# One core, attention with compressive memory beside a spectral filter: token-stage layout of W, folded back transform, merged masks, reciprocals through TensorE, and a new order

## The chip, the core and the metric

The kernel runs on one core of a Trainium2 chip. The core has five engines with a queue each: TensorE (PE, matrix products into the accumulation memory PSUM), VectorE (DVE), ScalarE (ACT), GpSimd (POOL) and SyncE (SP, which here only issues DMA transfers). Work memory is SBUF, 128 partitions wide. Inputs are in the chip's main memory (DRAM in the code). The metric is the device time of one execution in microseconds; lower is better. The kernel before takes 242.37 us, the median of three runs (241.94 to 242.49).

## The reference, cut to what matters

Two branches are computed from `x` (2048 tokens, width 640) and mixed by a gate per token:

```python
g = sigmoid((x * gate_w).sum(-1, keepdims=True))
# branch a: 32 heads of width 20, four segments of 512 tokens
for s in range(4):
    logits = einsum('bhqd,bhkd->bhqk', qs, ks) * scale + mask
    p = softmax(logits)
    a_dot = einsum('bhqk,bhkd->bhqd', p, vs)
    a_mem = einsum('bhld,bhde->bhle', phi(qs), M) / (einsum('bhld,bhd->bhl', phi(qs), z) + 1e-6)
    o = sigmoid(beta) * a_mem + (1 - sigmoid(beta)) * a_dot
    M, z = M + phi(ks)^T vs, z + sum(phi(ks))
a = o @ wo
# branch b
b = irfft2(rfft2(x) * (w_r + 1j * w_i))
out = g * a + (1 - g) * b
```

The mask is causal inside a segment. Softmax is done without its maximum: exponentials are taken, cells above the diagonal are set to zero, and the product with V carries a column of ones, whose result is the denominator.

## The kernel before

A recording layer (`Sched`) takes the whole kernel as some 2,000 operations, each with the buffers it reads and writes. The tuple `ORDER` says in which order they go to which engine, `ENDED` in which order they are thought to end; both are written out as numbers. Each engine then runs its own list strictly in order, and semaphores carry every dependence between engines. PSUM has eight banks: four for the scores of attention (`qk`), four for all else (`gen`). One scores unit takes all four `qk` banks, so the next unit's products start only when ACT has taken the exponentials of the one before.

Branch a, per segment `s`: `proj_tile` projects Q and K and sends them through main memory into a padded layout (`st_qk`, `pad`), `v_part` projects V, `qk_unit` makes scores in five units for a pair of head groups and takes their exponentials into `ex` (line 1393, ACT), and `mask` zeroes cells with POOL's affine select (line 1414), seven calls for each of 32 head groups, each as soon as its unit's exponentials are there. `pv_flipped` (segments 0 to 2) multiplies with V and sends the result, denominators included, to main memory (`st_u`, tile `u_scr`); `pv_group` does it for segment 3 without that detour. `mem_read_tile` reads the memory: a product, a denominator, a reciprocal and a multiplication for each half of the heads (lines 1281 to 1289, DVE). `denominators` (line 1331) loads the denominators back (`ld_den`), takes reciprocals on DVE (`den_rec`, line 1340), multiplies by the gate (`den_gate`, line 1342, tile `rc`) and stores them (`st_r`, tile `r_scr`). `finish_tile` then loads them back with each row repeated four times (`ld_r`, tile `r`), multiplies the attention result by them (`normal`, line 1656), adds the memory part (line 1664), and accumulates the product with `wo` (line 519) in the same PSUM bank as the last step of branch b.

Branch b, in `fft` (line 1495), is a two-dimensional real transform as matrix products. Stage F1 transforms over 128 of the token index. Stage D transforms over the width (tile `Bt`). Then comes the token stage, for 16 groups `g`: products T give real and imaginary parts, `W_mul` (line 1569, DVE) multiplies each of two PSUM results by `w_r` and `w_i` at once, `W_add` (line 1574, DVE or POOL) adds or subtracts the four products into `Yt`, and products Tb transform back, three chunks of the width by two, 256 columns each (tile `Cp`). The back transform over the width (Db) is, for each of 16 values of `n2` and for cosine and sine, three products of 321 columns; DVE adds and subtracts the two results into the two halves of `G` (`sum_Db`, line 1615), since cosine is even and sine is odd. The last step over the tokens (Fb) multiplies `G` by a table with the gate in it, into the bank of the `wo` product. Tables `tt` and the rows of W (`Wt`, double buffered, 32 transfers of 80 KB) come from main memory for each pair of groups.

SP issues nearly all transfers, in order; a transfer whose data are not ready holds all that stand behind it. All in all PE, DVE, ACT, POOL and SP run 1073, 481, 249, 293 and 232 recorded operations.

Of the kernel before, what the change touches and what calls it, by code (L numbers as in the profile page):

```python
# [8 lines left out]
ALU = mybir.AluOpType  # L9
# [35 lines left out]
class Op:  # L45
    __slots__ = ("id", "alts", "preds", "succs", "prio", "banks", "nbytes", "npred", "eng", "t0", "t1",
                 "stamp", "rank", "need_inc", "dyn", "first", "outside", "name", "dma", "key", "xfer", "lock", "mode", "emode", "hold", "width")


class Sched:  # L50
# [9 lines left out]
    def op(self, alts, r=(), w=(), prio=0.0, nbytes=0, name="", after=(), dma=False, xfer=0.0, lock=False, mode=0, hold=False, width=16):  # L60
# [3 lines left out]
        o = Op()  # L64
        o.id = len(self.ops)
# [46 lines left out]
    def schedule(self, pools, order, ended, nsem=56):  # L112
# [12 lines left out]
        for o in ops:  # L125
            o.dyn, o.t1 = [], None
            o.first = [b for b in o.banks if b.ops[0] is o]
            for b in o.banks:
                b.left = len(b.ops)
        pe, held = queue["pe"], {}  # L130
# [42 lines left out]
        def head(e):  # L173
# [4 lines left out]
            for p in o.preds:  # L178
                if p.t1 is None:
                    return None  # L180
                if p.eng != "pe" or e != "pe":
                    t = max(t, p.t1 + self.HOP)
            if o.first:
# [18 lines left out]
        while len(self.order) < len(order):  # L202
# [15 lines left out]
            o.t0 = t  # L218
            occ, lat = o.alts[e][1:]
# [95 lines left out]
def make_tables():  # L315
# [5 lines left out]
    for g in range(16):  # L321
        for i in range(4):
            a = 2 * pi * base_of(g, i) * n1 / 128
            F[:, g, i, 0], F[:, g, i, 1] = np.cos(a), -np.sin(a)
            Fp[g, i, 0], Fp[g, i, 1] = np.cos(a), np.sin(a)
# [23 lines left out]
    dd = np.arange(KD)  # L349
    IC = np.zeros((384, 322))  # L350
    IS = np.zeros((384, 322))
    IC[:KD, :KD] = ck[:, None] * np.cos(2 * pi * kd[:, None] * dd[None] / D)
    IS[:KD, :KD] = ck[:, None] * np.sin(2 * pi * kd[:, None] * dd[None] / D)
    IS[0] = 0
    IS[320] = 0
    IS[:, 320] = 0

    T = np.zeros((16, 128, 4, 128))
    Tp = np.zeros((16, 128, 2, 2, 16, 4, 2))
    n2 = np.arange(16)  # L360
    k2 = np.arange(16)
    for g in range(16):
        for half in range(2):
            for i in range(4):
                kb, pi_, kind, sg = pair_of(g, half, i)
                k = kb + 128 * k2
                ph = 2 * pi * np.outer(n2, k) / S
                c, s = np.cos(ph), np.sin(ph)
                m = half * 64 + k2 * 4 + i
                kr = n2 * 8 + pi_ * 2  # L370
                ki = kr + 1

                def put(t, rows, val):
                    T[g, rows[:, None], t, m[None, :]] = val
                if kind == "pair":
                    put(0, kr, c), put(0, ki, sg * s), put(1, kr, -s), put(1, ki, sg * c)
                    put(2, kr, -s), put(2, ki, sg * c), put(3, kr, -c), put(3, ki, -sg * s)
                else:
                    src = kr if kind == "zero" else ki
                    put(0, src, c), put(1, src, -s), put(2, src, -s), put(3, src, -c)  # L380

                def putp(r, typ, eo, val):
                    for q in range(16):
                        Tp[g, m[q], r, typ, :, pi_, eo] = val[:, q]
                if kind == "pair":
                    putp(0, 0, 0, c), putp(1, 0, 0, -s), putp(0, 0, 1, -sg * s), putp(1, 0, 1, -sg * c)
                    putp(0, 1, 0, -s), putp(1, 1, 0, -c), putp(0, 1, 1, -sg * c), putp(1, 1, 1, sg * s)
                else:
                    eo = 0 if kind == "zero" else 1
                    putp(0, 0, eo, c), putp(1, 0, eo, -s), putp(0, 1, eo, -s), putp(1, 1, eo, -c)  # L390

    def chunks(t):
        return np.ascontiguousarray(t.reshape(3, 128, -1).transpose(1, 0, 2))
    fcat = np.concatenate([F, np.eye(128), Fp], 1)
    inv = np.concatenate([chunks(IC), chunks(IS)], 1).reshape(128, 6 * 322)
    big = np.concatenate([dtab, inv], 1)
    hmask = np.zeros((128, 5, 8, VW))
    for t in range(5):
        for r in range(128):
            hmask[r, t, (128 * t + r) // DH - head0(t), :DH + 1] = 1.0  # L400
    b = ml_dtypes.bfloat16
    return {"fcat": fcat.astype(b), "big": big.astype(b),
            "tt": np.concatenate([T.reshape(16, 128, 512), Tp.reshape(16, 128, 512)], 2).astype(b),
            "hmask": hmask.reshape(128, 880).astype(b)}
# [7 lines left out]
def pair_of(g, half, i):  # L412

    if g == 0:
        if half == 0:
            return 32 * i, i % 2, ("zero", "pair", "nyq", "pair")[i], (1, 1, 1, -1)[i]
        return 16 + 32 * i, (3, 2, 2, 3)[i], "pair", (1, 1, -1, -1)[i]
    if half == 0:
        return g + 32 * i, i, "pair", (1, 1, -1, -1)[i]
    return 32 - g + 32 * i, 3 - i, "pair", (1, 1, -1, -1)[i]  # L420
# [48 lines left out]
class Kern:  # L469
# [79 lines left out]
    def dma(self, dst, src, nbytes, r, w, prio, tr=False, name="", after=(), queue="sp"):  # L549
# [13 lines left out]
        "ld_W": (620.0, 450.0, 16), "ld_beta": (400.0, 120.0, 16), "ld_big": (500.0, 2900.0, 16), "ld_den": (520.0, 150.0, 16),  # L563
        "ld_fcat": (400.0, 350.0, 16), "ld_g": (400.0, 1500.0, 16), "ld_gc": (580.0, 200.0, 16), "ld_gw": (420.0, 600.0, 16),
        "ld_hm": (600.0, 850.0, 16), "ld_r": (570.0, 500.0, 16), "ld_tt": (530.0, 1650.0, 16), "ld_u": (500.0, 450.0, 16),
# [4 lines left out]
        "st_part": (430.0, 250.0, 16), "st_r": (480.0, 200.0, 16), "st_u": (520.0, 700.0, 16), ("xT", 131072): (1240.0, 1300.0, 16), ("xT", 262144): (1700.0, 2300.0, 16),  # L570
# [1166 lines left out]
```

## Time and profile before

| what | before |
|---|---|
| device time, median of 3 runs | 242.37 us |
| the profiled execution: span, first to last instruction | 247.9 us |
| PE busy in the span | 230.0 us (93%) |
| DVE, ACT, POOL busy | 196.3, 199.7, 165.7 us |
| mean granted clock of TensorE | 0.972 |
| bytes moved by DMA | 42.11 MB |

The profile gives no time of the profiled execution beside its span; the span is 5.5 us longer than the median of the runs. A row of the page or of a view names a line of the code, the engine, the operation, the tile written and the tiles read, and how often; then come busy time and the mean of one in ns, and the idle time of the engine ahead of it with what ended it. Products overlap on PE, so the mean of one is longer than what one adds to a row of them. In the timelines the numbers are the start and the length in us of a stretch of equal instructions.

### The profile page before, as it was taken

Reading aid. Unit: us, or ns where it says so; the run is one execution under the profiler, and the core shown is the slowest. Engines: PE = TensorE matmul, PEld = TensorE weight load, DVE = VectorE, ACT = ScalarE, POOL = GpSimd, SP = SyncE. Lnnn points to the kernel's source line nnn. Section 1 sums busy time; section 2 is a strip of 40 time slices with the busy share of each in tenths; the row PEclk is TensorE's granted clock in tenths of the full one; section 3 lists DMA queues with packets and bytes.
Section 4 is the critical chain, followed back from the end, with each engine's and each line's share of the span. In section 5 each row is a group of like instructions: output and inputs, shape, how many; then the busy total and the mean of one; then the engine's idle time right before and its main releaser. Section 6 shows DMA issues by size and latency. Waiting matters only on the chain.

```text
span 247.9 us, 9233 instructions
## 1 busy us (share of the span) xinstructions
PE 230.0 (93%) x3849; PEld 139.7 (56%) x3849; DVE 196.3 (79%) x481; ACT 199.7 (81%) x241; POOL 165.7 (67%) x297
## 2 busy tenths in 40 slices
PE   7899999999999999998899999999999975699994
PEld 2574667765465665545566554455444543366794
DVE  0489998799999987888998979979888831755653
ACT  2289688998999989999999899999999864278740
POOL 8532278367969658478939998949898660559640
PEclk9999999999999999999999999999999995599999
DMA  7999979937875864768697543447665977382123
GB/s 174 281 361 206 229 191 230 269 91 203 222 173 163 199 213 114 206 95 252 170 242 208 165 131 99 122 146 192 188 183 128 282 101 81 35 118 81 59 81 109
DMA packets 58924, 42.11 MB, mean 170 GB/s; under 512 B 30020, under 2 KB 55172, under 8 KB 58884
## 3 DMA queue, kind: packets, MB, share of 16 engines
q1 hardware_dynamic: 57844, 40.96, 66.4%
q8 instruction: 30, 0.49, 0.8%
q10 hardware_dynamic: 1040, 0.57, 0.8%
q14 instruction: 10, 0.08, 0.2%
HBM read 23.32 MB, written 12.30 MB: 144 GB/s over the span
## 4 chain that ended last, share of the span: by engine, by line
PE 59%; DVE 15%; DMA 12%; ACT 8%; SPq 3%; issue 2%; DVEq 0%
PE psum L521 52%; PE psum L519 6%; ACT ex L1393 5%; DMA r<-r_scr 3%; DMA r_scr<-rc 3%; DVE Pt L1569 3%; DMA Wt<-in_B_w_i_dram 2%; DMA wk<-in_A_wk_dram 2%; DMA qk_scr<-qu 2%; SPq L553 2%; DVE G L1615 1%; SPq L555 1%; DVE oU L1656 1%; DVE phk L1213 1%; DVE va L1244 1%
## 5 line engine op out<-in xcount | busy, mean ns | idle before, releaser
L1393 ACT ACTIVATE ex<-psum 128x2048 bf16<-128x2048 f32 (+4 forms) x92 | 138.7, 1507 | 13.2 <-PE psum L521 11.4
L1414 POOL TENSOR_SCALAR_AFFINE_SELECT ex<-ex 128x256 bf16<-128x256 bf16 (+2 forms) x224 | 121.0, 562 | 41.2 <-ACT ex L1393 38.3
L521 PE MATMUL psum<-qkp 20*64 20x64 bf16 (+5 forms) x1024 | 31.8, 268 | 4.0 <-ACT ex L1393 2.1
L521 PE MATMUL psum<-xT,wk 128*128 128x256 bf16 (+1 forms) x280 | 33.9, 273 | 0.6 <-DMA wk<-in_A_wk_dram 0.6
L521 PE MATMUL psum<-xT,wq 128*128 128x512 bf16 (+1 forms) x135 | 30.7, 381 | 0.5 <-DMA xT<-in_A_x_dram 0.5
L521 PE MATMUL psum<-wv,xT 128*64 128x320 bf16 (+3 forms) x240 | 30.1, 303 | 0.3 <-DVE va L1244 0.3
L1569 DVE TENSOR_TENSOR Pt<-psum,Wt 128x642 bf16<-128x642 f32 x32 | 25.5, 821 | 2.6 <-PE psum L521 1.5
L521 PEld LDWEIGHTS psum<-qkp 20*64 20x64 bf16 (+1 forms) x1024 | 12.2, 101 | 22.0 <-ACT ex L1393 14.8
L521 PEld LDWEIGHTS psum<-xT,wk 128*128 128x128 bf16 (+1 forms) x280 | 19.9, 97 | 7.1 <-DMA wk<-in_A_wk_dram 1.6
L519 PE MATMUL psum<-wo,oU 128*32 128x320 bf16 x480 | 23.5, 317 | 0.2 <-DVE oU L1664 0.2
L1035 POOL TENSOR_TENSOR xsb<-xf 128x320 bf16<-128x320 bf16 (+2 forms) x12 | 9.5, 788 | 16.2 <-DVE xsb L1035 12.2
L1244 DVE TENSOR_TENSOR va<-psum,ebx 128x320 bf16<-128x320 f32 x32 | 15.2, 483 | 5.0 <-ACT gate L1242 2.9
L521 PEld LDWEIGHTS psum<-wv,xT 128*64 128x64 bf16 (+1 forms) x240 | 14.9, 105 | 7.4 <-issue 2.9
L532 DVE CAST ot<-psum 128x320 bf16<-128x320 f32 x21 | 10.1, 491 | 11.2 <-PE psum L519 8.8
L521 PE MATMUL psum<-big,Cp 128*128 128x321 bf16 (+1 forms) x96 | 18.7, 310 | 0.2 <-DVE G L1615 0.2
L521 PE MATMUL psum<-big,Ac 128*128 128x160 bf16 (+2 forms) x96 | 18.1, 257 | 0.3 <-DVE Pt L1569 0.2
L521 PE MATMUL psum<-ex,va 128*32 128x512 bf16 (+4 forms) x480 | 17.3, 275 | 0.5 <-DVE mem L1289 0.2
L521 PE MATMUL psum<-tt,Yt 128*128 128x256 bf16 (+1 forms) x96 | 16.5, 276 | 1.1 <-DVE Pt L1569 0.4
L1615 DVE TENSOR_TENSOR G<-eo,psum 128x320 bf16<-128x320 f32 x32 | 14.7, 482 | 3.5 <-PE psum L521 2.5
L1201 ACT ACTIVATE et<-qu 128x512 bf16<-128x512 bf16 x25 | 15.6, 629 | 0.2
L519 PEld LDWEIGHTS psum<-wo,oU 128*32 128x32 bf16 x480 | 12.5, 100 | 5.7 <-issue 1.1
L521 PEld LDWEIGHTS psum<-ex,va 128*32 128x32 bf16 x480 | 10.1, 96 | 9.8 <-POOL ex L1414 1.7
(99 smaller groups left out, 393.7 us busy)
## 6 DMA issues: line engine op xcount, KB each, us to landing
qkp<-qk_scr SPq DMA_DIRECT2D x28, 160.0 KB
tt<-tab_tt SPq DMA_DIRECT2D x8, 512.0 KB, 3.8
qk_scr<-qu SPq DMA_DIRECT2D x12, 256.0 KB, 2.4
u_scr<-ub SPq DMA_DIRECT2D x12, 256.0 KB, 4.4
xsb<-in_A_x_dram SPq DMA_DIRECT2D x8, 320.0 KB, 5.9
oU<-u_scr SPq DMA_DIRECT2D x15, 128.0 KB, 4.0
out_dram<-ot SPq DMA_DIRECT2D x12, 160.0 KB
Wt<-in_B_w_r_dram SPq DMA_DIRECT2D x16, 80.2 KB, 3.3
```

The lines of the kernel that those rows point to most:

```text
L519: h = e.matmul(dst, wt, r_, start=st, stop=sp_, **{**kw, "tile_position": (0, q), "skip_group_check": True})
L521: h = e.matmul(o_, l_, r_, start=st, stop=sp_, **kw)
L532: alts["dve"] = (lambda e: e.tensor_copy(dst(), src()), 67 + 1.04 * n, 68.0)
L553: return e.dma_start_transpose(d_, s_)
L555: return e.dma_start(d_, s_)
L1035: self.either(lambda e, dst=dst, src=src, d0=d0, n=n, op=op: e.tensor_tensor(xs.ap(o + dst, [D, 2], [1, n]), xf.ap(src + d0, [321, 2], [1, ...
L1201: self.one("act", lambda e: e.activation(et.ap(0, [1, L]), qsl(), ACT.Exp), L, [qb], [b("et", pi_)], late, name="phi_exp")
L1244: self.one("dve", lambda e: e.tensor_tensor(va.ap(i * H * VW + h0 * VW, [VW, nh], [1, DH]), self.ps(bank, 0, [DH, nh], [1, DH]), self.ebx. ...
L1393: self.one("act", lambda e, d=d, q=q: e.activation(self.ex.ap(*d), self.ps(bank, *q), ACT.Exp, scale=SC), n, [bank], [self.exb(s, 2 * pr + ...
L1414: self.one("pool", lambda e: e.affine_select(self.ex.ap(e0 + d0, [1280, 4], [1, n], np_=np_), self.ex.ap(e0 + s0, [1280, 4], [1, n], np_=np_),
L1569: self.one("dve", lambda e, ri=ri, Pt=Pt, Wt=Wt, wo_=wo_, bank=bank: e.tensor_tensor(Pt.ap(ri * 322, [644, 2], [1, KD]), self.ps(bank, 0, ...
L1615: self.one("dve", lambda e, q=q, n2=n2, bank=bank, eo=eo: e.tensor_tensor(self.G.ap(n2 * D + 639 * q, [1 - 2 * q, 320]), eo.ap(q, [1, 320] ...
```

## The change

1. **Token stage.** `W_add` and the tile `Yt` are gone. The tables are laid out so that real parts stand in partitions 0 to 63 and imaginary parts in 64 to 127; then the sums over real and imaginary parts happen inside the back products, which take the W products `Pt` themselves as weights: 192 products Tb of 128 columns in the place of 96 of 256, written in runs of four PSUM columns out of eight, with weights at every second column of `Pt`. The pairs of groups are ordered anew (`GROUPS`).
2. **W.** Both halves of the partitions need the same rows of W. They are loaded from main memory into partitions 0 to 63 and copied to 64 to 127 by one transfer inside SBUF (`dup_W`), which waits for the loads.
3. **Back transform.** Db is folded a second time: even and odd `kd` separately, 161 outputs each. Two products of 161 columns and one of 322 take the place of three of 321. `sum_Db` writes to a new f32 tile `UV`; a new operation `fold_Db` (32 times, DVE or POOL) makes `G` from it. Fb takes `G` in two pieces of 161 and 159 columns, the second backward: 256 products for 128.
4. **Masks.** Seven calls for a head group become four, made after all of its exponentials. Each covers two blocks; on DVE it is one `min` against a table of 0 and very large numbers, on POOL two affine selects. `ORDER` puts 66 of the 128 on DVE.
5. **Reciprocals.** `st_r`, `r_scr` and `ld_r` are gone. Four products with 0/1 tables spread `rc` over the partitions in PSUM (`spread`), and a copy brings it to SBUF (`ev_r`).
6. **Smaller ones.** `mem_read_tile` takes one reciprocal of 32 columns for two of 16. `phi_max` may run on POOL (15 of 30 do). The first piece of `wk` is issued by ACT's queue. `on` and `xf` lie elsewhere in SBUF; one of the fills of `va` comes after the folds.
7. **Order.** `ORDER` and `ENDED` are new throughout.

```diff
@@ mask
-        self.one("pool", lambda e: e.affine_select(
-            self.ex.ap(e0 + d0, [1280, 4], [1, n], np_=np_), self.ex.ap(e0 + s0, [1280, 4], [1, n], np_=np_),
...
+        least = lambda e: e.tensor_tensor(dst(), src(), self.hm.ap(880 + 64 * t, [0, 4], [0, 2], [1, 64], p0=p0, np_=np_), ALU.min)
+        def pick(e):
+            for d, q in ((d0, s0), (d1, s1)):
+                h = e.affine_select(self.ex.ap(e0 + d, [1280, 4], [1, 64], p0=p0, np_=np_), self.ex.ap(e0 + q, [1280, 4], [1, 64], p0=p0, np_=np_),
+                                    [[0, 4], [1, 64]], ALU.is_ge, 0.0, base=base, channel_multiplier=-1)
@@ qk_unit
-        for gp in gps:
...
+        if u == 3:
+            self.masks(s, 2 * pr, prio)
+        elif u == 4:
+            self.masks(s, 2 * pr + 1, prio)
@@ denominators
-        self.dma(lambda: dap(self.rd.ap(), s * H * L, [P, P], [1, P]), lambda: self.rc.ap(0, [1, P]), P * P * 2,
-                 [b("rc")], [b("rd", s)], prio, name="st_r")
+    def spread(self, s):
...
+        for t in range(4):
+            def th(t=t):
+                return self.ps(bank, t * P, [1, P]), self.hm.ap(1136 + t * P, [1, P]), self.rc[s].ap(0, [1, P]), t == 0, t == 3, {"skip_group_check": True}
+            items.append((th, P))
+        self.mms(items, [b("rc", s), b("hm"), bank], [], prio, name="spread", mode=0)
+        self.Sc.op(self.copy_alts(lambda: self.r4[s].ap(0, [1, L]), lambda: self.ps(bank, 0, [1, L]), L), r=[bank], w=[b("r4", s)], prio=prio,
+                   name="ev_r", after=[b("xT", 1, c) for c in range(5)])
@@ fft, token stage
-            for r, (a0, a1, op) in enumerate(((0, 3, ALU.subtract), (1, 2, ALU.add))):
-                fn = lambda e, r=r, a0=a0, a1=a1, op=op, Pt=Pt, Yt=Yt: e.tensor_tensor(
-                    Yt.ap(r * 322, [1, KD]), Pt.ap(a0 * 322, [1, KD]), Pt.ap(a1 * 322, [1, KD]), op)
...
+                            def th(c=c, r=r, x=x, Pt=Pt, tt=tt, to=to, bank=bank, np_=np_):
+                                rows = Pt.ap(x * 644 + r * 322 + (c if c < 2 else 256), [2 if c < 2 else 1, np_])
+                                return (self.ps(bank, c % 2 * 256 + 4 * x, [8, 32], [1, 4], np_=np_), rows, tt.ap(to + 512 + (2 * x + r) * P, [1, P]),
+                                        x == 0 and c % 2 == 0 and r == 0, r == 1, {"skip_group_check": True})
@@ fft, back transform over the width
+                        kc, n, o = (65, 322, 644 + typ * 322) if c == 2 else (P, 161, typ * 322 + c * 161)
...
+                fn = lambda e, q=q, n2=n2, uv=uv: e.tensor_tensor(
+                    self.G.ap(n2 * 644 + 322 * q, [161, 2], [1, 161]), uv.ap(0, [322, 2], [1, 161]), uv.ap(161, [322, 2], [1, 161]), ALU.subtract if q else ALU.add)
+                self.Sc.op({"pool": (fn, 120 + 2.2 * 322, 50.0), "dve": (fn, 67 + 1.04 * 322, 68.0)}, r=ub, w=[b("G", n2, q)], prio=prio, name="fold_Db",
+                           lock=True, after=acb)
@@ load_w (new)
+        rb = [b("Wt", wi, r, key) for r in range(2) for key in sorted({q[0] for q in parts})]
+        self.dma(lambda: Wt.ap(0, [1, 8 * KD], p0=64, np_=64), lambda: Wt.ap(0, [1, 8 * KD], np_=64), 64 * 16 * KD, rb, [b("Wt", wi, 0, 3), b("Wt", wi, 1, 3)], prio, name="dup_W")
@@ finish_tile
-                self.dma(lambda: self.r4[s].ap(0, [1, L]), lambda: dap(self.rd.ap(), s * H * L, [L, H], [0, 4], [1, L]), P * L * 2,
-                         [b("rd", s)], [b("r4", s)], prio - 9.0, name="ld_r", after=[b("xT", 1, c) for c in range(5)])
...
+                        rows = self.G.ap(o + (0, 322)[hf], [1, 161]) if n_ == 0 else self.G.ap(o + (483, 161)[hf] + 159, [-1, 159])
```

More of the change, by code (lines that the diff above doesn't have):

```diff
@@ L129, in schedule @@
                 b.left = len(b.ops)
+        for p, o in zip(queue["pool"], queue["pool"][1:]):
+            if p.high != o.high:
+                o.follow = p
         pe, held = queue["pe"], {}
@@ L182, in head @@
                     t = max(t, p.t1 + self.HOP)
+            if o.follow is not None:
+                t = max(t, o.follow.t1 + self.HOP)
             if o.first:
@@ L218, in schedule @@
             o.t0 = t
+            if o.follow is not None:
+                o.dyn.append(o.follow)
             occ, lat = o.alts[e][1:]
@@ L348, in make_tables @@
     ck = np.where((kd == 0) | (kd == 320), 1.0, 2.0) / (S * D)
[L349 to L359, printed above, removed]
-    n2 = np.arange(16)
[L361 to L367, printed above, removed]
+    dd = np.arange(161)
@@ L854, in TL @@
             late[0] += (shape[1] * mybir.dt.size(dtype) + 63) // 64 * 64
-            assert late[0] <= self.cur
+            assert late[0] <= (self.rc[0].off if late[0] < self.Wt[0].off else self.cur)
             return t
@@ L860, in alloc @@
         self.oU = [TL("oU0", [P, 5 * L])]
+        late[0] = self.Wt[0].off
         self.mT = [TL(f"mT{i}", [P, 5 * P]) for i in range(3)]
+        self.UV = [TL(f"UV{i}", [P, 644], F32) for i in range(2)]
         self.wq = T("wq", [P, 5 * D])
@@ L948, in record @@
         self.late_weights()
+        for s in range(3):
+            self.spread(s)
         for s in range(3):
@@ new lines, in mem_read_tile @@
+        self.one("dve", lambda e: e.reciprocal(dn.ap(32, [1, 32]), dn.ap(0, [1, 32])), 32, [b("dn", i % 2, q) for q in range(2)], [rb], prio, fix=145,
+                 name="mem_rec")
+        for q, bank in enumerate(banks):
+            if s < 3:
+                fn = lambda e, q=q, bank=bank: e.tensor_tensor(
+                    self.mem.ap(i * D + 64 * q, [4, 16], [P, 5], [1, 4]), self.ps(bank, 0, [VW, 16], [4, 5], [1, 4]),
+                    dn.ap(32 + 16 * q, [1, 16], [0, 5], [0, 4]), ALU.mult)
+            else:
+                fn = lambda e, q=q, bank=bank: e.tensor_tensor(
+                    self.mem.ap(i * D + q * 320, [DH, 16], [1, DH]), self.ps(bank, 0, [VW, 16], [1, DH]),
+                    dn.ap(32 + 16 * q, [1, 16], [0, DH]), ALU.mult)
+            self.one("dve", fn, 320, [bank, rb], [b("mem", i, q)], prio, name="mem_mul", after=[b("xf", 2)] if s == 1 else ())
@@ L1457, in pv_group @@
                 rs.ap(0, [4, 4], [1, 4], [0, DH]), ALU.mult), 320, [bank, rsb], [b("on", g)], prio, name="pv_mul",
-                after=[b("xf", k) for k in range(3)] if g == 0 else ())
+                after=[b("wv"), b("gw")] if g == 0 else ())
             if s > 0:
@@ L1597, in fft @@
             prio = tf(10.3 + 65.7 + 4.0 + n2 * 47.0 / 16)
+            eo, eb = self.eo[n2 % 3], b("eo", n2 % 3)
+            uv, ub = self.UV[n2 % 2], [b("UV", n2 % 2, q) for q in range(2)]
             for typ in range(2):
```

329 lines of the change are left out of this document (189 added, 140 removed), and 466 rows, old and new, of tables (ENDED, ORDER).

## The prediction

> **What bounds the kernel now.** First the page's totals, then the stretches of the span.
>
> ```profile
> span 247.9 us, 9233 instructions
> PE 230.0 (93%) x3849; PEld 139.7 (56%) x3849; DVE 196.3 (79%) x481; ACT 199.7 (81%) x241; POOL 165.7 (67%) x297
> ```
> ```profile
> core 0: us, PE busy (x) PEld busy (x) DVE busy (x) ACT busy (x) POOL busy (x), PEclk, DMA share, GB/s
> 0.00:12.00 12.00, 9.55 (x133) 4.56 (x134) 3.48 (x7) 2.78 (x5) 8.81 (x13) 1.00 0.89 223
> 40.00:160.00 120.00, 116.28 (x1686) 68.31 (x1683) 108.44 (x259) 112.59 (x128) 90.14 (x170) 1.00 0.68 178
> 160.00:200.00 40.00, 38.41 (x714) 21.69 (x715) 34.37 (x94) 36.62 (x46) 31.78 (x58) 1.00 0.72 186
> 200.00:220.00 20.00, 13.43 (x296) 8.04 (x294) 8.58 (x23) 9.34 (x12) 6.49 (x11) 0.66 0.65 80
> 220.00:235.00 15.00, 15.00 (x451) 10.16 (x444) 8.78 (x20) 11.91 (x15) 12.50 (x23) 1.00 0.27 74
> 235.00:248.00 13.00, 9.69 (x284) 8.84 (x280) 6.62 (x16) 3.22 (x6) 2.97 (x5) 1.00 0.31 91
> ```
>
> From 40 to 200 us PE is busy for 154.7 of 160 us, ACT for 149.2, DVE for 142.8: PE sets the pace, and the other two have little room. One stretch is unlike the rest: from 200 to 220 us every engine idles, and the granted clock is 0.66. The chain of waits says why, and PE's timeline with the stretch at half clock gives the price.
>
> ```profile
> 195.92 6.75 DMA r_scr<-rc
> 202.69 7.07 DMA r<-r_scr
> 209.78 1.77 DVE oU L1656 x5
> ...
> 213.43 1.26 PE psum L519 x16
> ```
> ```profile
> 202.61 0.43 PE L521 MATMUL psum<-qkp 20*64 20x512 bf16 x12 [1.79 <-DMA qkp<-qk_scr]
> ...
> 212.50 0.46 PE L521 MATMUL psum<-G,fbg 128*32 128x320 bf16 x4 [4.58 <-DVE on L1455]
> ```
> ```profile
> 203.80:217.40 13.60, 8.82 (x182) 5.31 (x177) 5.88 (x16) 5.33 (x7) 4.15 (x6) 0.50 0.59 71
> ```
>
> The reciprocals of segment 2 go to main memory and back, 6.75 and 7.07 us, and nothing else is left for PE by then. PE stands for 1.79 us (for a `pad`, not for the reciprocals). Then the clock halves: in 13.6 us PE is busy for 8.82, so it idles for 4.78 and loses half of 8.82, 4.41. Together 11.0 us are lost in this hole.
>
> **The sum.** It is made against the span of 247.9 us, 5.5 us over the median of the runs; I take the 5.5 off at the end. If the hole is shorter in the runs than in this execution, the gain is smaller by as much, which the range has to hold.
>
> *Reciprocals, −9.0.* The round trip is replaced by 4 products and a copy. What is late next is the reciprocal itself, and `spread` now stands in PE's own queue, so all of PE waits with it. Before, that part of the chain went so:
>
> ```profile
> 180.72 0.73 PE L521 MATMUL psum<-ex,va 128*32 128x512 bf16 x20 [0.20 <-DVE mem L1289]
> ```
> ```profile
> 182.29 0.56 SPq L555 DMA_DIRECT2D u_scr<-ub  x1
> ...
> 187.12 0.51 SPq L555 DMA_DIRECT2D dnc<-u_scr  x1
> ```
> ```profile
> 189.45 0.94 DVE L1340 RECIPROCAL dnr<-dnc 128x128 f32<-128x128 bf16 x1
> ...
> 192.65 0.47 DVE L1342 TENSOR_TENSOR rc<-dnr,gcc 128x128 bf16<-128x128 f32 x1
> ```
>
> From the end of the last `pvf` of segment 2 (181.45) to `rc` (193.12) are 11.7 us. In the new order PE has between these two points 18 steps of Db, 10 `wo` products, 4 `pv`, two Fb, two earlier spreads, and six score units. Each score unit waits for the exponentials of the one before:
>
> ```profile
> L1393 ACT ACTIVATE ex<-psum 128x2048 bf16<-128x2048 f32 x56 | 105.2, 1879 | 7.9 <-PE psum L521 6.7
> ```
>
> Six of 1.88 us are 11.3, with the hand-overs over 12: the reciprocal is just covered. The gap of 1.79 us for the pad is not touched by the change as such. If it stays and halves the clock, it leaves more: work began again at 213.43 and the clock was half until 217.4, 4 us, which cost 2. So 3.8 us may stay, or nothing: −7.2 to −11.0, and I take the middle. By the Trainium skill, page "TensorE: Matmul & The Clock Gate", section "Why this matters for your kernels", only an idle gap of about 3 us or more brings the half clock; here it was there 1.2 us behind a gap of 1.79. By the page's rule 1.8 would stay rather than 3.8.
>
> *Products, −3.0.* Db goes from 96 × 321 = 30,816 columns to 64 × 161 + 32 × 322 = 20,608; spreads add 12 × 128 = 1,536.
>
> ```profile
> 173.09 1.27 PE L521 MATMUL psum<-big,Cp 128*128 128x321 bf16 x8
> ...
> 179.76 0.44 PE L521 MATMUL psum<-big,Cp 128*128 128x321 bf16 x2
> ```
>
> Six more products take 0.83 us, so 0.138 each and 0.43 ns a column: 8,672 columns fewer are −3.7 us. PE's own order has 48 of its 64 Db steps behind the first scores of segment 3, where PE is the engine that is full, so most of it counts; bounds −3.7 and 0. Tb keeps its 24,576 columns in twice as many products. Their scattered writes and weights have no row in the trace. The nearest is the plain product of 128 columns:
>
> ```profile
> L521 PE MATMUL psum<-fcat,xsb 128*128 128x128 bf16 x80 | 7.9, 219 | 0.0
> ```
>
> That costs under 0.1 us with nothing lost ahead of it; if the scattered form went at half pace, 192 × 128 × 0.43 ns = +10.6 us. I take 0, since weight loads (PEld, 56% of the span) run beside products and have room. Fb has the same columns, four products abreast: 0.
>
> *DVE and POOL, +3.0.* Masks move from POOL to DVE, and folding adds work; W additions and half of `phi_max` leave.
>
> ```profile
> L1414 POOL TENSOR_SCALAR_AFFINE_SELECT ex<-ex 128x256 bf16<-128x256 bf16 x128 | 59.5, 476 | 38.7 <-ACT ex L1393 37.4
> L1414 POOL TENSOR_SCALAR_AFFINE_SELECT ex<-ex 64x512 bf16<-64x512 bf16 x64 | 42.6, 670 | 1.8 <-ACT ex L1393 0.9
> ...
> L1615 DVE TENSOR_TENSOR G<-eo,psum 128x320 bf16<-128x320 f32 x32 | 14.7, 482 | 3.5 <-PE psum L521 2.5 <-ACT eo L530 0.8
> ...
> L1574 DVE TENSOR_TENSOR Yt<-Pt 128x321 bf16<-128x321 bf16 x16 | 5.7, 380 | 0.0
> ...
> L1213 DVE TENSOR_SCALAR phq<-qu 128x512 bf16<-128x512 bf16 x15 | 5.3, 363 | 0.0
> ```
> ```profile
> L1214 DVE TENSOR_TENSOR phk<-phk,et x15: 361/416/882, 18.7 to 110.4; 128x512 bf16<-128x512 bf16 x15
> L1214 DVE TENSOR_TENSOR phq<-phq,et x15: 404/416/614, 38.7 to 162.7; 128x512 bf16<-128x512 bf16 x15
> ```
>
> A mask on DVE is a `min` of 512 bf16, as L1214 is: 66 × 0.416 = +27.5. 17 folds on DVE at 0.482 (the nearest, f32 of the same length): +8.2. W additions −5.7, 15 `phi_max` −5.4. Other counts move both ways by a few copies and are left out. DVE gains 24.6 us of work. It has 17.2 us free from 40 to 200, and 17.6 from 200 to 235. Crowding also shortens it:
>
> ```profile
> 156.65 0.81 DVE L1569 TENSOR_TENSOR Pt<-psum,Wt 128x642 bf16<-128x642 f32 x1
> ...
> 157.57 1.55 DVE L1569 TENSOR_TENSOR Pt<-psum,Wt 128x642 bf16<-128x642 f32 x2
> ```
>
> Two in a row take 1.55, not 1.62: 0.07 less, so the 83 added cost 5.8 less. 196.3 + 18.8 less 3.5 and 6.6 in the first 12 and last 13 us are 205 us, in a middle of 222.9 now: 92%, against 90% from 40 to 160. DVE fits, but PE will wait for it more often. Nothing is the lower bound; the upper is 18.8 less half of the 17.6 us free behind 200, +10. I take 3, nearer to the lower end because POOL, which slows DVE's instructions (416 against 882), loses a third of its work. The masks now start only when all exponentials of a group are there. On POOL one takes two selects of 0.476, so two take 1.9 us where the last three took 2 × 0.476 + 0.670 = 1.6: 0.3 later a group, hidden by the three buffers of `ex`; uncovered it were 32 × 0.3 = 9.6.
>
> *W, +1.0.* 38 loads and 8 copies replace 32 loads, 6 transfers of reciprocals go, and ACT takes one of `wk`: 7 more for SP. `dup_W` waits at the head of SP's queue, and stores of Q and K, pads and tables wait behind it.
>
> ```profile
> Wt<-in_B_w_r_dram SPq DMA_DIRECT2D x16, 80.2 KB, 3.3
> ```
>
> Four of the eight stand at most three issues behind their loads, some 1.2 us; a landing of 3.3 us then holds SP for 2.1, four times: 8.4 at most, 0 if pads come early enough. W has two buffers, one always a pair of groups ahead, so I take 1.
>
> *Start, −0.6.* The first piece of `wk` comes sooner; PE's two waits for it go, 0 at worst:
>
> ```profile
> 6.51 0.62 PE L521 MATMUL psum<-xT,wk 128*32 128x256 bf16 x16 [0.20 <-DMA wk<-in_A_wk_dram]
> ...
> 11.74 1.27 PE L521 MATMUL psum<-xT,wk 128*128 128x256 bf16 x10 [0.41 <-DMA wk<-in_A_wk_dram]
> ```
>
> ACT takes eight more final copies and a few others, mostly after 200 us where it has room, and memory reads lose 12 reciprocals on DVE: 0.
>
> Sum: −9.0 − 3.0 + 3.0 + 1.0 − 0.6 = −8.6, so a span of 239.3 and a time of **233.8 us**; its own range is 229 to 238.
>
> **The rivals.** *The hole comes back under another name* (0.20). `spread` is in PE's queue, and the 11.7 us of its chain are hardly more than covered. If loads of denominators or pads land late, behind `dup_W` or the loads of `wo`, PE stands some 3 us and runs at half clock for 4: 5 us more, 238.8. For it speaks that two landings in this stretch took 7 us each; against it that the chain lost two transfers.
>
> *Everything covered* (0.16). The good ends of all bounds: −11.0 − 3.7 − 0.6 = −15.3, a time of 227.1. Against it stands the load of DVE.
>
> *Masks make DVE the bound* (0.09, slower). DVE and POOL now mask side by side. L1214 took 0.416 in the middle but up to 0.614 for `phq` and 0.882 for `phk`. If the 66 masks took 0.614, DVE had 13.1 us more on a path already full: 233.8 + 13.1 = 246.9. It is slower than before from 0.416 + 8.6/66 = 0.546 us a mask on. Against it: the middle of thirty such instructions is 0.416 with POOL at 67%. The Trainium skill, "GPSIMD Engine Reference", section "Key points", says that POOL shares its SBUF interfaces with DVE and contends with DVE instructions of two SBUF inputs, which a mask on DVE is. The longest ones above agree with that.
>
> *Scattered Tb at half pace* (0.04, slower): 233.8 + 10.6 = 244.4.
>
> **How the numbers follow.** The forecast has 0.51. The three faster cases make 0.87; 0.11 goes to slower by more than 0.2% (about what a measurement of this kernel tells from no change, 0.5 us), 0.02 to what lies between. The range reaches from just under the best case to the old time: 226 to 242.
>
> **What would show it.** Right: no row of `r_scr`; a granted clock of 1.00 from 40 us to the end; PE busy over 95% in the last 60 us; DVE near 215 busy; masks on DVE near 0.42 us; Db steps of 0.14 us. Wrong: PE waiting for `rc` or `qkp` over 2 us in the last 70 us, DVE masks over 0.55, Tb products over 0.1 us apart, ACT idle for PE or POOL in the middle, or SP held by `Wt`.

## The result and the profile after

The changed kernel takes 256.10 us (median of 4 runs, 255.81 to 256.39) against 242.16 us before (241.92 to 242.49): a ratio of 1.0577, 95% interval 1.0562 to 1.0593. It is slower by 13.9 us, where 233.8 us and a gain were predicted, and outside the range of 226 to 242.

First the page of the changed kernel: its span, and busy time, share and instructions of each engine.

```profile
span 254.6 us, 9691 instructions
...
PE 230.3 (90%) x4072; PEld 146.9 (58%) x4085; DVE 222.2 (87%) x531; ACT 205.0 (81%) x250; POOL 120.8 (47%) x201
```

Then its stretches, with the columns of the table shown of before (busy time of PE, of PE's weight loads, of DVE, ACT and POOL, then the granted clock).

```profile
core 0: us, PE busy (x) PEld busy (x) DVE busy (x) ACT busy (x) POOL busy (x), PEclk, DMA share, GB/s
0.00:12.00 12.00, 9.45 (x148) 4.97 (x149) 2.45 (x6) 2.86 (x4) 2.78 (x8) 1.00 0.89 217
40.00:160.00 120.00, 114.77 (x1820) 72.26 (x1830) 114.61 (x264) 112.39 (x122) 77.12 (x137) 1.00 0.77 195
160.00:200.00 40.00, 32.80 (x516) 19.16 (x513) 36.19 (x88) 32.65 (x40) 17.35 (x29) 0.74 0.58 160
200.00:220.00 20.00, 18.12 (x437) 11.08 (x441) 18.04 (x43) 14.24 (x18) 7.64 (x11) 0.83 0.52 102
220.00:240.00 20.00, 19.08 (x581) 13.34 (x570) 19.41 (x48) 15.87 (x24) 7.68 (x11) 1.00 0.35 91
```

DVE has 222.2 us of work, 26 more than before, and is busy 188.3 of the 200 us from 40 to 240 (94%). The loss shows from 160 us on. There PE is busy for 32.8 of 40 us, where it had 38.4 before, and the clock drops. Ahead of the last products there are three stretches at half clock, 27.3 us in all; the profiled execution of before had one of 13.6 us:

```profile
168.05:171.47 3.42, 3.42 (x48) 1.61 (x40) 3.10 (x11) 2.79 (x4) 3.17 (x6) 0.50 0.33 68
181.71:198.77 17.06, 14.77 (x221) 8.80 (x221) 14.97 (x34) 12.72 (x16) 5.97 (x10) 0.50 0.59 168
209.01:215.84 6.83, 6.08 (x104) 3.17 (x100) 6.08 (x14) 2.71 (x4) 2.54 (x3) 0.50 0.50 50
```

What PE waits for ahead of the second of them is told by three timelines of the changed kernel, of PE, DVE and POOL (start, length, instructions; in brackets the idle time ahead and what ended it).

```profile
178.03 0.73 PE L551 MATMUL psum<-ex,va 128*32 128x512 bf16 x20 [0.97 <-DVE ex L1508]
...
182.05 0.94 PE L551 MATMUL psum<-ex,va 128*32 128x512 bf16 x8 [1.74 <-DVE ex L1508]
```
```profile
176.66 1.77 DVE L1508 TENSOR_TENSOR ex<-ex,hm 64x512 bf16<-64x512 bf16 x3
178.46 1.01 DVE L1707 TENSOR_TENSOR UV<-eo,psum 128x322 f32<-128x322 f32 x2
179.39 0.42 DVE L1508 TENSOR_TENSOR ex<-ex,hm 128x512 bf16<-128x512 bf16 x1
179.72 1.05 DVE L1711 TENSOR_TENSOR G<-UV 128x322 bf16<-128x322 f32 x1
180.69 1.30 DVE L1508 TENSOR_TENSOR ex<-ex,hm 128x512 bf16<-128x512 bf16 x2
```
```profile
176.82 0.87 POOL L1711 TENSOR_TENSOR G<-UV 128x322 bf16<-128x322 f32 x1 [2.05 <-DVE UV L1707]
...
179.55 1.83 POOL L1711 TENSOR_TENSOR G<-UV 128x322 bf16<-128x322 f32 x2 [0.41 <-DVE UV L1707]
```

The half clock of 181.71 sets in while PE stands in the second of these gaps (180.31 to 182.05). The products with V wait for masks (`ex`, L1508) that DVE has not come to: its row has no gap, and masks, sums of Db and folds take turns in it. Beside POOL's folds DVE's own instructions are longer: its fold at 179.72 took 1.05 us. The Trainium skill, "GPSIMD Engine Reference", section "Specifications", has such contention for DVE instructions with two SBUF inputs, and the trace agrees. The groups of the changed kernel (busy us, mean ns, idle time ahead) give the usual lengths:

```profile
L1512 POOL TENSOR_SCALAR_AFFINE_SELECT ex<-ex 128x256 bf16<-128x256 bf16 x64 | 27.0, 449 | 26.9 <-DVE ex L1508 13.0 <-ACT ex L1476 11.2 <-ACT qu L560 2.1
...
L1508 DVE TENSOR_TENSOR ex<-ex,hm 128x512 bf16<-128x512 bf16 x32 | 16.1, 511 | 0.2
L1279 POOL TENSOR_SCALAR phq<-qu 128x512 bf16<-128x512 bf16 x8 | 15.8, 1970 | 0.6 <-ACT qu L560 0.6
L1508 DVE TENSOR_TENSOR ex<-ex,hm 64x512 bf16<-64x512 bf16 x34 | 15.0, 443 | 1.2 <-ACT ex L1476 0.6
L1279 POOL TENSOR_SCALAR phk<-qu 128x512 bf16<-128x512 bf16 x7 | 13.4, 1918 | 2.7 <-DMA pkn<-phk 2.5 <-DVE qu L562 0.2
L551 PE MATMUL psum<-tt,Pt 128*128 128x128 bf16 x128 | 10.6, 219 | 0.4 <-DVE Pt L1663 0.3
L1711 DVE TENSOR_TENSOR G<-UV 128x322 bf16<-128x322 f32 x17 | 10.5, 620 | 0.1
L1279 DVE TENSOR_SCALAR phq<-qu 128x512 bf16<-128x512 bf16 x7 | 2.1, 303 | 0.0
L551 PE MATMUL psum<-rc,hm 128*128 128x128 bf16 x12 | 1.6, 281 | 0.0
```

A `phi_max` (L1279) takes 1.92 to 1.97 us on POOL and, for `phq`, 0.30 on DVE.

### The profile page after: what moved, and what is told of

It reads as the page before. It is cut to its first block, busy times and chain, and to the rows that moved or that the text cites. A ratio compares the mean times of both kernels' runs of the same rounds, so it can differ in the third digit from the quotient of the medians.

```text
span 254.6 us, 9691 instructions
## 1 busy us (share of the span) xinstructions
PE 230.3 (90%) x4072; PEld 146.9 (58%) x4085; DVE 222.2 (87%) x531; ACT 205.0 (81%) x250; POOL 120.8 (47%) x201
## 4 chain that ended last, share of the span: by engine, by line
PE 43%; DVE 25%; ACT 16%; DMA 5%; issue 3%; POOL 3%; ACTq 2%; SPq 1%; DVEq 0%
PE psum L551 39%; ACT ex L1476 11%; DVE ex L1508 5%; PE psum L549 4%; DVE UV L1707 3%; DVE G L1711 3%; DMA qk_scr<-qu 2%; DMA xT<-in_A_x_dram 2%; DVE xsb L1101 2%; ACTq L585 2%; DVE xf L1096 2%; DVE va L1310 2%; DVE oU L1780 1%; ACT et L1267 1%; DVE oU L1772 1%
## 5 line engine op out<-in xcount | busy, mean ns | idle before, releaser
L1512 POOL TENSOR_SCALAR_AFFINE_SELECT ex<-ex 128x256 bf16<-128x256 bf16 (+1 forms) x124 | 53.4, 458 | 56.7 <-ACT ex L1476 33.3
L1508 DVE TENSOR_TENSOR ex<-ex,hm 128x512 bf16<-128x512 bf16 (+1 forms) x66 | 30.5, 476 | 1.4 <-ACT ex L1476 0.6
L551 PE MATMUL psum<-wv,xT 128*64 128x321 bf16 (+3 forms) x240 | 26.9, 301 | 1.0 <-DVE va L1310 1.0
L551 PE MATMUL psum<-xT,wq 128*128 128x512 bf16 (+1 forms) x122 | 24.8, 380 | 1.6 <-issue 0.5
L549 PE MATMUL psum<-wo,oU 128*32 128x320 bf16 x480 | 24.3, 337 | 1.1 <-DVE oU L1780 0.9
L1711 POOL TENSOR_TENSOR G<-UV 128x322 bf16<-128x322 f32 x15 | 13.4, 907 | 19.6 <-DVE UV L1707 18.1
L551 PE MATMUL psum<-big,Cp 128*128 128x161 bf16 (+1 forms) x96 | 16.8, 301 | 1.3 <-DVE UV L1707 1.3
L560 ACT ACTIVATE ot<-psum 128x320 bf16<-128x320 f32 x19 | 8.1, 436 | 11.4 <-PE psum L551 5.2
L1707 DVE TENSOR_TENSOR UV<-eo,psum 128x322 f32<-128x322 f32 x32 | 15.3, 486 | 2.1 <-PE psum L551 1.6
L551 PE MATMUL psum<-tt,Pt 128*128 128x128 bf16 (+1 forms) x192 | 16.5, 220 | 0.4 <-DVE Pt L1663 0.3
L1279 POOL TENSOR_SCALAR phq<-qu 128x512 bf16<-128x512 bf16 x8 | 15.8, 1970 | 0.6 <-ACT qu L560 0.6
```

The costliest lines, as they stand in the source:

```text
L549: h = e.matmul(dst, wt, r_, start=st, stop=sp_, **{**kw, "tile_position": (0, q), "skip_group_check": True})
L551: h = e.matmul(o_, l_, r_, start=st, stop=sp_, **kw)
L560: alts["act"] = (lambda e: e.activation(dst(), src(), ACT.Copy), 65 + 0.833 * n, 110.0)
L1279: fmax = lambda e: e.tensor_scalar(dst(), qsl(), 0.0, 1.0, ALU.max, ALU.add)
L1508: least = lambda e: e.tensor_tensor(dst(), src(), self.hm.ap(880 + 64 * t, [0, 4], [0, 2], [1, 64], p0=p0, np_=np_), ALU.min)
L1512: h = e.affine_select(self.ex.ap(e0 + d, [1280, 4], [1, 64], p0=p0, np_=np_), self.ex.ap(e0 + q, [1280, 4], [1, 64], p0=p0, np_=np_), [[0, ...
```

## The experiments

Each run is given as its ratio to the kernel before on the same chip; the changed kernel has 1.058. The theories: D, DVE's load sets the pace; G, short gaps of PE and the half clock behind them; P, the slow `phi_max`; F, POOL's folds; W, the copy of W; H, no hole in the timed runs; O, the order.

**The kernel before once more**, unchanged.

> The kernel before, unchanged, to see whether the hole at 200 to 220 us (11.0 us lost, the source of the largest term of the sum) is in the timed executions too. Theory H (the hole was longer in the profiled execution than in the timed ones): spans of 240 to 241 us in the timed executions, a mean clock of 0.985 or more, and at most 4 us of the hole left; then the term of -9.0 was mostly not there to be gained. Rival (the hole is always there and 5.5 us lie elsewhere): spans near 247, mean clock 0.972.

242.74 us, ratio 1.0002 (0.9953 to 1.0051). Its page, its stretches, and the longest step of the reciprocals in its chain of waits (start, length):

```profile
span 241.0 us, 9233 instructions
...
PE 227.7 (94%) x3849; PEld 138.9 (58%) x3849; DVE 197.2 (82%) x481; ACT 199.1 (83%) x241; POOL 166.2 (69%) x297
```
```profile
40.00:160.00 120.00, 116.79 (x1700) 68.97 (x1697) 109.44 (x260) 113.00 (x129) 91.11 (x173) 1.00 0.69 178
160.00:200.00 40.00, 38.39 (x715) 21.87 (x718) 34.29 (x95) 36.51 (x46) 31.75 (x58) 1.00 0.77 189
200.00:220.00 20.00, 18.21 (x510) 11.88 (x498) 12.78 (x31) 15.38 (x18) 13.86 (x23) 1.00 0.77 97
```
```profile
198.38 3.78 DMA r<-r_scr
```

H holds. Here `r` lands in 3.78 us instead of 7.07, PE idles for 1.8 us from 200 to 220, and the clock is 1.00. The other timed executions of this run look the same: spans of 240 to 244 us, clocks of 0.993 to 1. The hole of 11 us belonged to one execution.

**All `phi_max` on DVE.**

```diff
             o.eng = list(o.alts)[v % 2]
+            if o.name == "phi_max":
+                o.eng = "dve"
```

> The changed kernel with all 30 phi_max on DVE, everything else in its place. Theory P (15 phi_max on POOL take 1.92 us each where DVE takes 0.28, 29 us in POOL's queue that no term of the sum held; what waits behind them makes the kernel slow): 243 to 249 us, granted clock over 0.97. Theory D (DVE is full from 165 us on, PE starves behind its masks, folds and products, and the clock halves): DVE gets 4.2 us more, 255 to 259 us, three stretches at half clock as before. Theory F (folds on POOL hold DVE's instructions up): as D.

255.82 us, ratio 1.0507 (1.0405 to 1.061). P's 243 to 249 us did not come. POOL has 29 us less to do, DVE 1.4 us more instead of 4.2, and the time is the same within the interval: P is not the cause. The time lies in D's range, but with so little more on DVE that says little for D.

**The masks of segment 3 on POOL** (`outside` holds the segment of a mask)**, and the folds on DVE.**

```diff
+            if o.outside == 3:
+                o.eng = "pool"
```
```diff
+            if o.name == "fold_Db":
+                o.eng = "dve"
```

> The changed kernel with the 24 masks of segment 3 that were on DVE moved to POOL in their place of the order (two selects each, about 0.92 us against 0.42). Theory D: DVE loses 10 us of work after 188 us, PE no longer starves there, the half clock of 209 to 216 goes: 248 to 253 us. Theory P: nothing there is changed, 255 to 257. Rival to both (POOL's queue in this order is then too slow, 22 us more in 50 us): 258 to 268.

262.15 us, ratio 1.0751 (1.0661 to 1.084).

> The changed kernel with the 15 fold_Db that were on POOL moved to DVE in their place of the order. Theory F (each fold of f32 on POOL stretches the DVE instruction beside it by some 0.55 us, 5.4 us in all between 177 and 222 us): DVE gets 15 x 0.41 = 6 us and is rid of 5.4, PE waits less for G: 251 to 255 us. Theory D: DVE gets 6 us more where it is full already: 258 to 263 us. Theory P: 255 to 258.

257.71 us, ratio 1.0589 (1.0469 to 1.0709). With the masks on POOL, D's 248 to 253 us did not come but the rival to both theories: in this order POOL is too slow for them. PE waits 3.1 us for POOL's masks (0.3 in the changed kernel), and DVE has only 4.4 us less (217.8), since its 17 folds now take 0.83 us on average where they took 0.62. With the folds on DVE the time did not change. F's gain is missing. D's loss is too, but DVE is busy for only 0.8 us more (222.2 to 223.0 by the page): a fold takes 0.53 us on average instead of 0.62, and the 66 masks 29.2 us instead of 31.1. So the run does not speak against D.

**W loaded into both halves, without the copy.**

```diff
-        self.dma(lambda: Wt.ap(0, [1, 8 * KD], p0=64, np_=64), lambda: Wt.ap(0, [1, 8 * KD], np_=64), ... name="dup_W")
+        for up in range(2):
...
+                    p0 += 64 * up
```

> The changed kernel without the copy of W inside SBUF: each half of the partitions is loaded from main memory (76 loads for 38 and 8 copies), the loads of the upper half at the place of the copy, so that nothing waits at the head of SP's queue for W. Theory W (SP held by the copy, 5.5 us in all, makes pads and tables late): 2 to 5 us off, a ratio to the kernel before of 1.037 to 1.050 (the changed kernel has 1.058). Theories G and D: SP is not on the path, ratio 1.053 to 1.065.

261.48 us, ratio 1.073 (1.0611 to 1.0848): slower. W's gain did not come, but the edit does not only take the copy away: it puts 30 more issues on SP, and PE then waits 5.6 us for `Pt`, 0.9 in the changed kernel. So the run sets 30 loads against the copy and does not price the copy alone. In the trace of the changed kernel SP waits 5.8 us for `Wt` in all, and its chain of waits has one load of W, 2.60 us at 114.70; the only transfer that ends a wait of PE there is `xT` at the start (1.4 us). That speaks against W without settling it.

**Idle products in PE's gaps**, alone and with all `phi_max` on DVE.

```diff
+            th = lambda: (self.ps(bank, 0, [1, 512]), self.fcat.ap(P, [1, P]), self.big.ap(0, [1, 512]), True, True, ...)
+        self.fill({(2, 5): 5, (2, 6): 6, (2, 7): 9}.get((s, g), 0), bank, prio)
         self.mms(items, self.exall(s, g) + ... name="pvf", mode=2)
```

> The changed kernel with four runs of idle products of 512 columns (5, 6, 9 and 7 of them, results overwritten) on PE, ahead of the three products with V of segment 2 and the one scores unit for which PE stood 0.86, 0.97, 1.74 and 1.38 us between 166 and 186 us. Nothing comes sooner by it, PE only does not idle. Theory G (short gaps between 164 and 187 us drop PE's busy share, and the half clock that follows, 27 us of it, slows everything behind): the half clock of 168 and 182 to 199 us goes, 7 to 10 us off, ratio 1.015 to 1.03. Theory D (DVE is the pace, the half clock costs nothing where PE waits anyway): within 1.5 us of the changed kernel, ratio 1.05 to 1.065.

255.62 us, ratio 1.0532 (1.0454 to 1.061). The stretches that were left at half clock, in the windows of this run:

```profile
194.60:201.50 6.90, 6.58 (x110) 3.83 (x112) 6.27 (x15) 4.72 (x9) 3.35 (x7) 0.51 0.29 85
208.30:215.10 6.80, 6.40 (x123) 3.59 (x126) 6.73 (x16) 3.73 (x4) 3.41 (x3) 0.50 0.24 35
```

> The same idle products, and all phi_max on DVE as in the run before (which had a ratio of 1.051). If the half clock and the slow phi_max add up (theories G and P): 1.4 us less than with the idle products alone, or more, since 165 us of the run with phi_max on DVE were in time; ratio 1.00 to 1.025. Theory D: DVE has 4.2 us more, ratio 1.05 to 1.065.

253.91 us, ratio 1.048 (1.0393 to 1.0567). Both runs cut the half clock ahead of the last products from 27.3 to 13.7 us, and the time stayed within what is measured. The gain that G gave for this is missing: with DVE's full load, 222.5 us in a span of 254.7 in the first run, this half of the half clock costs nothing that the runs tell. The other 13.7 us stood in both runs.

**Half of the masks' work left out.**

```diff
+        if t:
+            half = lambda d: self.ex.ap(e0 + d, [1280, 4], [1, 64], p0=p0, np_=np_)
+            least = lambda e: e.tensor_tensor(half(d0), half(s0), self.hm.ap(880 + 64 * t, [0, 4], [1, 64], p0=p0, np_=np_), ALU.min)
```

> The changed kernel with the 45 masks on DVE that work in place cut to one of their two blocks (the other block is left unmasked): about 0.28 for 0.42 us, 6 us of DVE's work less. Theory D (what DVE has to do between 165 and 225 us is what PE waits for): 6 to 12 us off, the half clock shorter than 27 us, ratio 1.01 to 1.035. Theory G without D (the gaps come from the order, not from DVE's load): less than 3 us off, ratio over 1.045.

250.20 us, ratio 1.0319 (1.0224 to 1.0413). Its page:

```profile
span 248.4 us, 9704 instructions
...
PE 227.0 (91%) x4085; PEld 145.3 (59%) x4085; DVE 216.1 (87%) x531; ACT 204.5 (82%) x250; POOL 118.1 (48%) x201
```

DVE has 6.1 us less to do (222.2 to 216.1), and the span is 6.2 us shorter (254.6 to 248.4). D holds in this order, about one for one (2.6 points of the ratio, the run's interval is 0.9 to each side). The work taken off is masks, though, for which PE waits; the run does not tell a shorter mask from a smaller sum.

**DVE's load put into the kernel before.**

```diff
-            self.Sc.op({"dve": (fmin, ...)}, r=[b("et", pi_)], w=[db], prio=late, name="phi_min", lock=True)
+            for name in ("phi_min", "again"):
+                self.Sc.op({"dve": (fmin, ...)}, r=[b("et", pi_)], w=[db], prio=late, name=name, lock=True)
...
+                    for name in ("sum_Db", "again"):
```

> The kernel before, in its own order, with 62 more instructions on DVE that repeat the one ahead of them to the same result (each phi_min and each sum_Db twice): some 25 us more of DVE's work, about what the change adds (197 to 222 us), and nothing else of the change. Theory D (the added load on DVE is the cause): DVE at 95% from 40 us on, 8 to 15 us slower, ratio 1.03 to 1.065. Theory O (the order and its waits are the cause; DVE of before idles for 44 us and can take it): under 4 us, ratio up to 1.017.

270.65 us, ratio 1.1157 (1.1105 to 1.1208): more than D gave. Its page and two stretches:

```profile
span 268.7 us, 9294 instructions
...
PE 239.5 (89%) x3849; PEld 141.1 (53%) x3849; DVE 227.4 (85%) x543; ACT 201.2 (75%) x241; POOL 167.9 (62%) x297
```
```profile
40.00:160.00 120.00, 109.78 (x1575) 64.05 (x1572) 111.39 (x263) 102.39 (x118) 81.73 (x154) 0.99 0.66 171
160.00:200.00 40.00, 34.84 (x464) 18.21 (x457) 38.17 (x92) 32.52 (x37) 29.50 (x54) 0.92 0.45 127
```

30.2 us more on DVE (197.2 to 227.4) made the span 27.7 us longer (241.0 to 268.7), although DVE idled for 43.8 us before; it still idles for 41.3. That idle time was no room. (A repeat writes the tile of the instruction that it repeats, so whoever reads the tile waits for the repeat as well. The price holds this delay beside the load, and the run does not separate them.)

**DVE's load taken out of the changed kernel.**

```diff
+        if t:
+            col = lambda d: self.ex.ap(e0 + d, [1280, 4], [d1 - d0, 2], [1, 1], p0=p0, np_=np_)
+            least = lambda e: e.tensor_tensor(col(d0), col(d0), ..., ALU.min)
...
+            fmin = lambda e: e.tensor_tensor(few(), few(), et.ap(0, [1, 8]), ALU.min)
```

> The changed kernel, in its own order, with the 45 masks on DVE that work in place cut to one column of a block and phi_min cut to 8 columns (masks and phi_min are left out but for these): about 20 us of DVE's work less, so that DVE has as little as before (197 to 202 us). Theory D: the slope of the run with half masks (6.2 us of span for 6.1 us of DVE's work) goes on until PE sets the pace: 238 to 244 us, ratio 0.985 to 1.005. Theory O: what the order costs stays, 246 to 252 us, ratio 1.015 to 1.04.

247.74 us, ratio 1.0213 (1.0165 to 1.026). Its page:

```profile
span 245.4 us, 9704 instructions
...
PE 226.1 (92%) x4085; PEld 144.6 (59%) x4085; DVE 203.1 (83%) x531; ACT 204.0 (83%) x250; POOL 116.4 (47%) x201
```

19.1 us of DVE's work less took 9.2 us off the span. The first six, masks alone, paid in full, the rest a quarter. Of that rest some 8 us are `phi_min`, all ahead of 163 us, where PE was busy for 114.8 of 120 us and had little to gain. Against the kernel before, DVE still has 5.9 us more and the span is 4.4 us longer. By the ratio, 3.6 points of the 5.8 go with DVE's load. The rest lies between 160 and 200 us:

```profile
160.00:200.00 40.00, 32.14 (x601) 18.73 (x600) 36.35 (x99) 35.31 (x44) 17.49 (x31) 0.87 0.62 168
```

There PE idles for 7.9 us, 1.6 in the second profile of before, and DVE is as full as in the changed kernel (36.4 and 36.2 of 40 us; 34.3 before). So the run lightened DVE over the whole, but not in this stretch. Two runs were to tell what the other 2.1 points are.

> The run with little work on DVE (masks in place cut to one column of a block, phi_min to 8 columns; ratio 1.021) and all phi_max on DVE besides, 4 us more for DVE. Theory R (the 5 us that were left over are the slow phi_max on POOL and the half clock, 10 us of it): 1 to 3 us off, ratio 1.008 to 1.017. Theory O (the order itself costs them, by many short waits): no change or 1 to 4 us more, since DVE has 4 us more, ratio 1.018 to 1.037.

247.17 us, ratio 1.0194 (1.0126 to 1.0262). The interval holds the 1.0213 of the run before it and reaches into R's 1.008 to 1.017, so this run does not tell the two theories apart.

> As the run beside it, with the four runs of idle products on PE besides, so that the clock stays up between 165 and 190 us. Theory R: no half clock but at the end, 2 to 5 us less than the run beside it, ratio 0.99 to 1.007. Theory O, and what the idle products showed with the full load on DVE (nothing gained): within 1.5 us of the run beside it.

249.46 us, ratio 1.0293 (1.0239 to 1.0346). R's gain did not come, but its condition did not come either: the idle products moved the half clock without shortening it. Ahead of the last products it is 13.7 us in both profiles, from 178.8 to 189.0 and 199.3 to 202.7 us without them, from 187.3 to 194.1 and 204.4 to 211.2 with them. So these runs do not show what the half clock costs; the 2.3 us more with the idle products lie at the edge of the intervals.

**Another order**, for the changed kernel and for the one before. Only the numbers in `ORDER` and `ENDED` differ.

> The operations of the changed kernel in another order, found by moving single operations between places and engines under the kernel's own planning rules, with phi_max on POOL priced at the measured 1.9 us and with a penalty on stretches where PE has little to do. DVE then has 26 phi_max, 72 masks and 16 folds, so no less work than before. Theory D (DVE's load, 222 us of 255, is what makes the changed kernel slow): still slower than the kernel before, ratio 1.01 to 1.045. Theory O (only the order is at fault, fitted to a wrong price of phi_max): ratio 0.975 to 1.00.

259.80 us, ratio 1.0732 (1.0652 to 1.0812): slower than D gave, and far from the 0.975 to 1.00 of O. DVE has 227.4 us in this order.

> The operations of the kernel before, none changed, in an order found in the same way. It tells what a fresh order is worth by itself, which is a part of the change too. If the order of before is as good as it gets on the chip: ratio 0.997 to 1.01. If a search for the order gains as much as its planner says: 2 to 4 us, ratio 0.983 to 0.992, faster than both kernels.

250.23 us, ratio 1.0343 (1.0268 to 1.0419): neither of the two. Its page:

```profile
span 248.7 us, 9212 instructions
...
PE 226.6 (91%) x3837; PEld 139.0 (56%) x3849; DVE 203.4 (82%) x489; ACT 198.0 (80%) x233; POOL 168.1 (68%) x297
```

The order found for the kernel before gave DVE eight instructions that ACT had (x489 for x481, ACT x233 for x241) and 6.2 us more to do, and the span is 7.7 us longer. So here an order that is better by the planner's prices lost 3% on the chip, and what the new order of the change is worth by itself could not be told. No kernel tried here beats the one before.

## Why the prediction was wrong, point by point

*"DVE fits" and "I take 3"* is the step that failed most. It read DVE's idle time (17.2 us from 40 to 200, 17.6 behind) as room for 24.6 us of work. The load was 7 us over the forecast: DVE busy is 222.2, where 215 were forecast and 197.2 are in the second profile of before. Masks took 0.47 us for 0.416 and folds 0.62 for 0.482, together 5.9 us more. The price was further off: 3.6 points of the ratio, 8.8 us, went with 19.1 us of DVE's work, and 6.2 us of span with the first 6.1; in the old order 30.2 us cost 27.7. As the timelines between 176 and 182 us show, DVE takes its work in order, and PE, waiting for one mask, waits for all that stands ahead of it. The bound of +10 may have been too low as well: if the other terms came as forecast, 13.9 + 1.8 + 3.0 − 1.0 + 0.6 = 18.3 us are left for DVE and the order together (1.8 for the reciprocals, from below).

*"Reciprocals, −9.0"*: the mechanism came as told. There is no row of `r_scr`, and `spread` has no idle time ahead of it (0.0 in its row). The size was wrong, because the hole was that of one execution. The second profile of before has 1.8 us of idle PE in that stretch and a clock of 1.00, so 1.8 was the most that could be gained there. The prediction saw the sign, a span 5.5 us over the median of the runs, and took the 5.5 off at the end; but the gain of 9.0 lay mostly in those same microseconds and should have been struck with them. Span and time are not the same, either: the second profile has a span of 241.0 us and a time of 242.98, so the first execution was some 6.9 us longer (247.9 − 241.0), not 5.5. With 1.8 in the place of 9.0 the sum would still have given some 241 us, so this term explains the missing gain and not the loss.

*The rival "Masks make DVE the bound"* named the right engine, with the wrong condition. It was to decide from 0.546 us a mask; the 66 masks took (16.1 + 15.0)/66 = 0.47 on average, and the kernel was slower all the same. That the sum of DVE's work counts, and not the length of a mask alone, is borne out by the old order with `phi_min` and `sum_Db` doubled, which has no masks on DVE; in the changed kernel no run separates the two. Its time of 246.9 is too low for the same reason as the forecast.

*"Products, −3.0"*: Tb costs what a plain product costs (219 ns, 0.4 us of waiting; 18 in a row at 159.79 us take 1.18 us), so the +10.6 of half pace did not come. But PE did not set the pace any more: it idles for 24.3 us of the span (254.6 − 230.3), 13.3 in the second profile of before, and 27 idle products on it cost nothing while DVE had its full load. What became of the 3 us, no run shows by itself.

*"W, +1.0"*: SP's wait of 5.8 us for `Wt` is inside the bound of 8.4. No run shows what it cost; the run without the copy was slower, but had 30 more loads to issue.

*`phi_max`* on POOL was counted only as 5.4 us off DVE. The instruction takes 1.92 us there, 29 us in all, which the prediction never priced. It cost little: the ratio went from 1.058 to 1.051 without it, which the intervals do not tell from nothing.

*The signs*: "a granted clock of 1.00 from 40 us" failed from 168 us on, and PE was busy for 52.3 of the last 60 us (87%), not over 95%. DVE near 215 was 222.2. Of the signs of "wrong" two came, both weakly: SP was held by `Wt` for 5.8 us, and ACT waited for PE for 11.6 us from 40 to 200, 8.1 before. The others looked for long masks, slow Tb products and waits for `rc`. What each microsecond on DVE costs, none of them measured.

Left open: what holds the changed kernel at 2% over the old one when DVE's work is cut to nearly the old sum. It lies between 160 and 200 us, where DVE stayed full, where the order brings masks, sums and folds together, and where the clock was 0.87; no run separates these three.

## What to carry to other kernels

Idle time of an engine that works in order, and for whose results others wait, need not be room: here DVE idled for 44 of 241 us, and doubling 62 of its instructions cost nearly their own length. Look at the stretch in which the work falls, too: of the last 13 us taken off DVE, most of them ahead of 163 us, where PE was full, only a quarter was gained. Before a stall is counted as a gain, compare the span of its execution with the timed ones, and strike what they don't share. An operation that moves to another engine needs a price on that engine, from a row, or else as an unknown with bounds.

## What the runs showed of the hardware that was not expected

`max` and `add` with two constants on 128x512 bf16 took 1.91 to 2.16 us on POOL and some 0.3 on DVE, while POOL's select of 128x256 took 0.45 on average.

The half clock came in stretches of 3.42, 6.83 and 17.06 us, and 13.60 in the first profile of before: about 1, 2, 5 and 4 times 3.41. The Trainium skill, "TensorE: Matmul & The Clock Gate", section "Part 1: The HAM clock gate", has a window of 3413 ns, and the trace agrees. The long gap of about 3 us, which the prediction drew from that page, was not needed: ahead of 181.71 PE had stood for 0.97 us, then for 0.38, and for 1.40 of a gap of 1.74 that was not yet over; in the last 3.42 us it was busy for 1.64.

DVE's fold is stretched beside POOL's. The rows of this line in the changed kernel (least, median and longest in ns):

```profile
L1711 DVE TENSOR_TENSOR G<-UV x17: 478/489/1079, 175.3 to 231.0; 128x322 bf16<-128x322 f32 x17
L1711 POOL TENSOR_TENSOR G<-UV x15: 751/872/1284, 170.4 to 232.0; 128x322 bf16<-128x322 f32 x15
```

Half take 0.49 us or less; the one at 179.72, beside two of POOL's, took 1.05. With no fold on POOL their mean is 0.53 us for 0.62, and with 24 masks more on POOL it is 0.83.
